# A two-bank PSUM tile becomes two one-bank tiles, allocated at each use

## The chip, the cores and the metric

The kernel runs on one core of one Trainium2 chip. The metric is the device time of one execution in microseconds (us), the median of several runs. A profile of one execution says where the time goes. The engines are TensorE (PE; its weight loads are PEld), VectorE (DVE), ScalarE (ACT), GpSimd (POOL) and SyncE (SP), which here only issues DMAs.

## The reference

Two branches work on 2048 tokens of 576 features and are mixed by a gate:

```python
g = sigmoid((x * gate_w).sum(-1, keepdims=True))
# branch A: a spectral filter
X = rfft2(x, axes=(-2, -1)) * (w_r + 1j * w_i)
a = irfft2(X, s=(2048, 576))
# branch B: a gated MLP, 576 -> 4608 -> 576
b = (gelu(x_b @ w_gate) * (x_b @ w_up)) @ w_down
out = g * a + (1 - g) * b
```

## The kernel before

*The MLP.* It is done in float32 precision by splitting each operand into a high and a low part and adding three products. The 4608 hidden features are 36 tiles of 128, taken in 18 pairs (j even, j odd); the tokens are two halves of two blocks (`tb`) of 512. For a hidden tile, `chain(j, s, tb)` adds 14 matmuls of 128x512 into one PSUM bank (512 float32 numbers a partition), for the gate (s=0) and for the up projection (s=1). `hidden` calls them one after the other: gate chain, `act.activation(..., Gelu_apprx_tanh)` on ScalarE out of the gate's bank (line 796), up chain, then VectorE's multiply out of the up's bank (`mult`, line 800), ScalarE's copy of the product to `hb` (high part) and VectorE's subtraction for the low part (line 804). `down` multiplies `hb` by `dn` (w_down) into the double tile `pdn`, 12 matmuls of 128x288 (line 818); ScalarE scales it to `stg` (line 843), and GpSimd issues a DMA that adds it to `yd` in DRAM. The downs of a hidden pair come one step later, four of them beside each pair of chains.

*The last stage.* For the second half of the tokens and the last 14 pairs of hidden tiles, `products` computes the gate and up projections by seven products of sums of blocks (Strassen's scheme) in place of eight. Each of the seven, n = 0 to 6, has two parts s of 7 matmuls (`seven`, lines 1013 to 1016), and VectorE adds each part out of PSUM to what it belongs to (`add`, line 1048). For odd n the parts go into `px`, by `ps_one()`, which takes the halves in turn; for even n into `pgu`.

*The transform.* The spectral filter runs in pieces beside the MLP: VectorE does the butterflies, and `columns` does DFTs over the columns by matmul (`product`, line 272, 6 matmuls of 128x290, three for each half al), between the chains, some 220 us from 350 on. There `wide[0]` is False and the chains use `pgu` alone; elsewhere the chains of an even j use `px`.

*PSUM.* There are eight banks: `pgu` is one bank in two buffers, `pdn` two banks in two buffers, and `px` one tile of two banks, allocated once at the beginning. `px` serves `first_chains` (the first pair), the chains of even j, the column products, the products of odd n, and `ps_one()` once more in `finale`.

*Order.* The order of instructions on each engine is that of the program text. `gap()`, called at fixed places in the chains, downs and products, emits queued work: steps due after so many gaps (`at`, `seq`), and pieces of the transform as far as a credit of estimated microseconds goes (`tick` adds what a chain takes on TensorE, the pieces subtract). Neither depends on measured time. The framework sets the semaphores: an instruction waits for those that touched the same tile before it, and where a tile is allocated anew under a name (tag), its first writer waits until the last tile in that buffer is free.

Of the kernel before, what the change touches and what calls it, by code (L numbers as in the profile page):

```python
# [10 lines left out]
F32 = mybir.dt.float32  # L11
F32R = mybir.dt.float32r
AF = mybir.ActivationFunctionType
ALU = mybir.AluOpType

P = 128
# [4 lines left out]
NK = KF + 1  # L21
# [4 lines left out]
TB = 512  # L26
# [132 lines left out]
def _build(nc, tc, a):  # L159
    with ExitStack() as ctx:  # L160
        ctx.enter_context(tc.manual_schedule())
        pool = ctx.enter_context(tc.tile_pool(name="sb", bufs=1))
        psum = ctx.enter_context(tc.tile_pool(name="ps", bufs=1, space=bass.MemoryType.PSUM))
        vec, act, pl, pe = nc.vector, nc.scalar, nc.gpsimd, nc.tensor

        def mk(n, shape, dt=F32):
            return pool.tile([P] + shape, dt, name=n, tag=n)
# [9 lines left out]
        gu = [mk(f"gu{i}", [2, KT, 256], F32R) for i in range(3)]  # L177
# [19 lines left out]
        def ps_gu():  # L197
            return psum.tile([P, TB], F32, name="pgu", tag="pgu", bufs=2)
# [1 line left out]
        def ps_dn():  # L200
            return psum.tile([P, 2, 512], F32, name="pdn", tag="pdn", bufs=2)

        px = psum.tile([P, 2, 512], F32, name="px", tag="px", bufs=1)
        ones = [0]

        def ps_one():
            ones[0] += 1
            return px[:, ones[0] % 2]

        def copy(o, i):  # L210
            act.activation(o, i, AF.Copy)  # L211
# [11 lines left out]
        def two(x):  # L223
            return x.rearrange("p (c k) -> p c k", c=2)[:, :, 0:NK]
# [3 lines left out]
        def columns():  # L228
# [5 lines left out]
            Z = [st[q] for q in turn]  # L234
# [4 lines left out]
            def cc(s, kb):  # L239
                q = 1024 * s + 512 * (kb % 2)  # L240
                return colm[:, q:q + 512]

            def load_cc(s, kb):
                if kb < 16:
                    pl.dma_start(cc(s, kb), a["col"][s, turn[kb]])

            def load_ww(kb):
                if kb < 16:
                    for c in range(2):
                        nc.sync.dma_start(ww[kb % 2][c], a["wf"][turn[kb], c])  # L250

            def corner(kb, slot, back):

                if not 0 <= kb < 16:
                    return
                z, c = two(Z[kb]), cns[:, slot + kb % 2]
                if back:
                    nc.sync.dma_start(z[0:64, 1], c[0:64])
                    nc.sync.dma_start(z[64:128, 0], c[64:128])
                else:  # L260
                    nc.sync.dma_start(c[0:64], z[64:128, 0])
                    nc.sync.dma_start(c[64:128], z[0:64, 1])

            def low(l, x, h):
                vec.tensor_tensor(l, x, f(h), ALU.subtract)

            def product(d, kb, h, l):
                v = px
                c = cc(d, kb).rearrange("p (a l k) -> p a l k", a=2, l=2)
                for al in range(2):  # L270
                    for n, (q, x) in enumerate(((0, h), (1, h), (0, l))):
                        pe.matmul(v[:, al, :NK], c[:, al, q], two(x)[:, al], start=n == 0, stop=n == 2)
                tick(6 * 0.135)
                load_cc(d, kb + 2)
                return v
# [48 lines left out]
            v = w = None  # L324
            for kb in range(18):
                on, was = kb < 16, 1 <= kb < 17
                if kb < 16:
                    z, (w0, w1) = two(Z[kb]), ww[kb % 2]
                    zr, zi = z[:, 0], z[:, 1]

                def filter_start():
                    vec.tensor_tensor(zi, v[:, 0, :NK], zr, ALU.subtract)
                    vec.tensor_tensor(zr, v[:, 0, :NK], zr, ALU.add)

                def swap():
                    act.activation(vs2[0:64], z[64:128], AF.Copy, scale=-1.0)
                    copy(vs2[64:128], z[0:64])

                def filter_end():
                    vec.tensor_tensor(z, z, two(vs), ALU.add)  # L340
                    vec.tensor_tensor(vs2[:, 0], zr, zi, ALU.add)
                    vec.tensor_tensor(vs2[:, 1], zr, zi, ALU.subtract)

                for g in range(STEP):
                    if g == 0:
                        while kb % 4 == 2 and kb < 14 and made[0] < kb // 4 + 1:
                            credit[0] -= next(side[0])
                        if on:
                            v = product(0, kb, xh, xl)
                            load_ww(kb + 1)  # L350
                            corner(kb + 2, 0, False)
                        if was:
                            copy(yh, vs)
                    elif g == 1:
                        if on:
                            copy(zr, v[:, 1, :NK])
                        if kb + 1 < 16:
                            copy(xh2, two(Z[kb + 1]))
                        corner(kb - 2, 2, True)
                    elif g == 2:  # L360
                        if on:
                            filter_start()
                        if was:
                            low(yl, vs, yh)
                    elif g == 3:
                        if on:
                            swap()
                            corner(kb + 2, 0, True)
                        if kb + 1 < 16:
                            low(xl2, two(Z[kb + 1]), xh2)  # L370
                    elif g == 4:
                        if was:
                            w = product(1, kb - 1, yh, yl)
                            copy(two(Z[kb - 1]), w[:, :, :NK])
                        if on:
                            vec.tensor_tensor(z, z, two(w0), ALU.mult)
                            vec.tensor_tensor(vs, vs, w1, ALU.mult)
                    elif g == 5:
                        if on:
                            filter_end()  # L380
                        if was:
                            corner(kb - 1, 2, False)
                    if kb == 17 and g > 4:
                        break
                    credit[0] -= 5.45 / STEP if on else 0.0
                    gone[0] = kb * STEP + g
                    yield None
# [254 lines left out]
        def tick(us):  # L642
            credit[0] += RATE * us
# [75 lines left out]
        def due(key):  # L719
            q = todo.pop(key, [])  # L720
            while q:
                q.pop(0)()
# [28 lines left out]
        wide = [True]  # L751

        def chain(j, s, tb):
            due(("gu", j))
            ps, w = px[:, s] if wide[0] and j % 2 == 0 else ps_gu(), gu[j % 3]
            c = slice(s * P, (s + 1) * P)
            for k in range(4):
                pe.matmul(ps, w[:, 0, k, c], xhi[tb][:, k], start=k == 0, stop=False)  # L758
                pe.matmul(ps, w[:, 1, k, c], xhi[tb][:, k], start=False, stop=False)  # L759
                pe.matmul(ps, w[:, 0, k, c], xlo[tb][:, k], start=False, stop=False)  # L760
                tick(3 * 0.2265)
                if k in (0, 2):
                    gap()
            pe.matmul(ps, w[:, 0, 4, c], xtl[tb], start=False, stop=False)  # L764
            pe.matmul(ps, w[:, 1, 4, c], xtl[tb], start=False, stop=True)  # L765
            tick(2 * 0.2265)
            return ps

        def first_chains():

            ps = [px[:, c] for c in range(2)]
            w, cs = gu[0], (slice(0, P), slice(P, 2 * P))
            for k in range(KT):
                for l, x in ((0, xhi), (1, xhi), (0, xlo)) if k < 4 else ((0, xtl), (1, xtl)):
                    for s in range(2):
                        x0k = x[0][:, k] if k < 4 else x[0]
                        pe.matmul(ps[s], w[:, l, k, cs[s]], x0k, start=k == 0 and l == 0 and x is xhi,
                                  stop=k == 4 and l == 1)
                tick(6 * 0.2265)
                if k < 4:  # L780
                    gap()
            return ps
# [237 lines left out]
        def products(i, spare, pend):  # L1020
# [31 lines left out]
            for n, (name, nd) in enumerate(zip(("a11", "a12", "s2", "s3", "s1", "a22", "s4"), downs)):  # L1052
# [9 lines left out]
                if n == 4:  # L1062
                    due(("dn", j))
                    due(("dn", j + 1))
                    load_d(i + 1)
                ps = [ps_one() if n % 2 else ps_gu() for _ in range(2)]
                for s in range(2):
                    seven(ps[s], i, n, name, s)
# [61 lines left out]
        ps = ps_gu()  # L1130
# [55 lines left out]
        for n in range(4 * NBLK):  # L1186
            p, r = divmod(n, 2 * NBLK)
            i, tb = divmod(r, 2)
            j = 2 * (p * NBLK + i)
# [21 lines left out]
            if state == 2 and tb == 1:  # L1211
                w = [g.rearrange("p l t k -> p (l t k)") for g in (gu[(j + 2) % 3], gu[j % 3], gu[(j + 1) % 3])]
# [95 lines left out]
```

## Time and profile before

| | |
|---|---|
| median of 3 runs | 1499.36 us (1496.73 to 1501.07) |
| profiled execution | 1502.38 us, span 1500.6 us |
| mean granted TensorE clock | 0.993 |
| PE busy | 1396.9 us of matmuls, 7490 of them |
| DVE busy | 1122.5 us |
| ACT busy | 701.7 us |
| POOL busy | 266.3 us |
| HBM | 118.56 MB read, 99.61 MB written |

The span is the time from the first to the last instruction on the core; the execution's own time is 1.8 us longer. Busy is the time in which an engine had an instruction in work. A matmul's row is longer than the distance to the next one's start, since matmuls are pipelined. In the rows of the timeline stand start (us), length (us), engine, line, operation, output<-input, shapes, count, and in brackets the idle time of the engine just ahead and what it waited for. In the rows of waits stand the engine with the waiting instruction's output and line, whom it waited for, and us in total, times, and the longest.

### The profile page before, as it was taken

What the parts mean: (1) busy time and instruction counts of PE and PEld (TensorE: products, weight loads), DVE (VectorE), ACT (ScalarE), POOL (GpSimd) and SP (SyncE); (2) the same over time, 40 slices, a digit from 0 to 9 for tenths busy, and PEclk for the clock granted to TensorE, in tenths of its full rate; (3) what the DMA queues carried; (4) which work ended last, traced back from release to release, by engine and by line L of the source; (5) the groups of instructions that cost most, each with busy time, mean ns of one, the idle gap of its engine ahead of it and who ended that gap; (6) DMA issues with size and microseconds to landing.
All of it is one profiled execution on the core that took longest, in us unless ns stands there. A gap on an engine that the chain in (4) does not pass through costs nothing. (4 is left out here: it accounts for less than half of the span.)

```text
span 1500.6 us, 20072 instructions
## 1 busy us (share of the span) xinstructions
PE 1396.9 (93%) x7490; PEld 1207.0 (80%) x7490; DVE 1122.5 (75%) x1649; ACT 701.7 (47%) x1079; POOL 266.3 (18%) x326
## 2 busy tenths in 40 slices
PE   9999999999999999999998989899999999999997
PEld 7778788888889878888887878777777787777787
DVE  6889798987877776998888841766666766666765
ACT  5443334355555664434644384444444444444441
POOL 0011111122222211111320022111111111111110
PEclk9999999999999999999999999999999999999999
DMA  9476655668999976557694777666665666666666
GB/s 335 160 177 140 146 118 96 113 124 192 216 237 271 249 153 124 106 105 141 129 280 139 202 155 121 147 121 118 119 120 111 108 114 110 106 114 121 115 133 158
DMA packets 102226, 226.65 MB, mean 151 GB/s; under 512 B 12400, under 2 KB 22640, under 8 KB 101744
## 3 DMA queue, kind: packets, MB, share of 16 engines
q0 software_dynamic: 45248, 92.56, 40.7%
q1 hardware_dynamic: 56880, 132.81, 28.1%
q8 instruction: 59, 0.97, 0.3%
q14 instruction: 39, 0.32, 0.1%
HBM read 118.56 MB, written 99.61 MB: 145 GB/s over the span
## 5 line engine op out<-in xcount | busy, mean ns | idle before, releaser
L831 POOL DMA_DIRECT2D yd<-stg x264 | 230.1, 872 | 1141.9 <-ACT stg L843 1101.4
L843 ACT ACTIVATE stg<-pdn,omg 128x576 f32<-128x576 f32 x272 | 201.9, 743 | 443.3 <-PE pdn L818 328.3
L818 PEld LDWEIGHTS pdn<-dn,hb 128*128 128x128 f32 x2760 | 382.1, 188 | 11.8 <-DVE raws L872 0.5
L818 PE MATMUL pdn<-dn,hb 128*128 128x288 f32 x2760 | 389.8, 295 | 0.2 <-DVE raws L872 0.2
L758 PE MATMUL pgu<-xhi,gu 128*128 128x512 f32 x440 | 172.8, 393 | 2.6 <-ACT gl L796 2.6
L759 PE MATMUL pgu<-xhi,gu 128*128 128x512 f32 x440 | 172.4, 392 | 0.4 <-DMA gu<-lo 0.4
L760 PE MATMUL pgu<-xlo,gu 128*128 128x512 f32 x440 | 172.1, 391 | 0.0
L758 PE MATMUL px<-xhi,gu 128*128 128x512 f32 x256 | 106.3, 415 | 37.3 <-ACT gl L796 37.3
L211 ACT ACTIVATE gu<-raws 128x1280 fp32r<-128x1280 f32 (+3 forms) x84 | 86.2, 1026 | 57.2 <-PE px L764 45.6
L759 PE MATMUL px<-xhi,gu 128*128 128x512 f32 x256 | 103.2, 403 | 0.0
L760 PE MATMUL px<-xlo,gu 128*128 128x512 f32 x256 | 102.8, 402 | 0.0
L760 PEld LDWEIGHTS pgu<-xlo,gu 128*128 128x128 f32 x440 | 83.0, 189 | 18.1
L758 PEld LDWEIGHTS pgu<-xhi,gu 128*128 128x128 f32 x440 | 83.0, 189 | 17.8 <-ACT gl L796 3.0
L758 PEld LDWEIGHTS px<-xhi,gu 128*128 128x128 f32 x256 | 49.5, 193 | 59.4 <-ACT gl L796 50.8
L759 PEld LDWEIGHTS pgu<-xhi,gu 128*128 128x128 f32 x440 | 83.0, 189 | 15.7 <-DMA gu<-lo 0.8
L818 PEld LDWEIGHTS pdn<-dn,gu 128*128 128x128 f32 x672 | 92.2, 188 | 2.1
L818 PE MATMUL pdn<-dn,gu 128*128 128x288 f32 x672 | 93.5, 295 | 0.0
L796 ACT ACTIVATE gl<-pgu 128x512 f32<-128x512 f32 x55 | 32.8, 597 | 125.5 <-PE pgu L765 111.8
L804 DVE TENSOR_TENSOR hb<-gl,hb 128x512 fp32r<-128x512 f32 x88 | 60.4, 686 | 40.9 <-ACT hb L211 40.6
L1048 DVE TENSOR_TENSOR xraw<-gl,px 128x512 f32<-128x512 f32 x56 | 38.5, 688 | 60.8 <-PE px L1016 58.3
L1013 PE MATMUL px<-xhi,gu 128*128 128x512 f32 x112 | 47.2, 421 | 27.3 <-DVE xraw L1048 27.3
L1031 DVE TENSOR_TENSOR xraw<-xraw 128x512 f32<-128x512 f32 x56 | 38.8, 693 | 31.5 <-ACT xraw L1039 30.9
(220 smaller groups left out, 2678.3 us busy)
## 6 DMA issues: line engine op xcount, KB each, us to landing
yd<-stg POOLq DMA_DIRECT2D x264, 288.0 KB, 5.0
raws<-wgu SPq DMA_DIRECT2D x42, 640.0 KB, 5.5
raws<-wd SPq DMA_DIRECT2D x72, 288.0 KB, 2.9
quads<-ws SPq DMA_DIRECT2D x24, 384.0 KB, 4.3
colm<-col POOLq DMA_DIRECT2D x32, 256.0 KB, 6.3
raws<-ws SPq DMA_DIRECT2D x21, 384.0 KB, 5.1
lo<-gu SPq DMA_DIRECT2D x8, 640.0 KB, 3.9
gu<-lo SPq DMA_DIRECT2D x8, 640.0 KB, 5.7
```

Of the source, the lines that this page charges most:

```text
L211: act.activation(o, i, AF.Copy)
L758: pe.matmul(ps, w[:, 0, k, c], xhi[tb][:, k], start=k == 0, stop=False)
L759: pe.matmul(ps, w[:, 1, k, c], xhi[tb][:, k], start=False, stop=False)
L760: pe.matmul(ps, w[:, 0, k, c], xlo[tb][:, k], start=False, stop=False)
L796: act.activation(g, pg, AF.Gelu_apprx_tanh)
L804: vec.tensor_tensor(h[:, 1], g, f(h[:, 0]), ALU.subtract)
L818: pe.matmul(ps[half], h[:, l, c], d[:, q, half * HD:(half + 1) * HD], start=part == 0 and n == 0, stop=part == 1 and n == 2)
L831: pl.dma_start(yd[u], o, accum_op=ALU.add)
L843: put(u, lambda o: act.activation(o.rearrange("p (c k) -> p c k", c=2), v[:, :, 0:HD], AF.Copy, scale=omg[:, u:u + 1]), i == 0)
L1013: pe.matmul(ps, hi[:, c], xh[:, t], start=t == 0, stop=False)
L1031: vec.tensor_tensor(v, g, v, ALU.mult)
L1048: vec.tensor_tensor(o, x, v, ALU.add)
```

## The change

The tile `px` of two banks goes. In its place `ps_x(c)` allocates a tile of one bank, under the name px0 or px1, at each use: for each chain of an even j, for the two halves of each column product, for each part of the products of odd n (by `ps_one`), and for the first pair. The banks used are the same two, in the same turns. A column product is now a list of two tiles, so ScalarE's copy of both halves in one instruction becomes two copies.

```diff
-        px = psum.tile([P, 2, 512], F32, name="px", tag="px", bufs=1)
+        def ps_x(c):
+            return psum.tile([P, TB], F32, name=f"px{c}", tag=f"px{c}", bufs=1)
+
         ones = [0]
 
         def ps_one():
             ones[0] += 1
-            return px[:, ones[0] % 2]
+            return ps_x(ones[0] % 2)
...
            def product(d, kb, h, l):
-                v = px
+                v = [ps_x(c) for c in range(2)]
...
-                        pe.matmul(v[:, al, :NK], c[:, al, q], two(x)[:, al], start=n == 0, stop=n == 2)
+                        pe.matmul(v[al][:, :NK], c[:, al, q], two(x)[:, al], start=n == 0, stop=n == 2)
...
-                    vec.tensor_tensor(zi, v[:, 0, :NK], zr, ALU.subtract)
-                    vec.tensor_tensor(zr, v[:, 0, :NK], zr, ALU.add)
+                    vec.tensor_tensor(zi, v[0][:, :NK], zr, ALU.subtract)
+                    vec.tensor_tensor(zr, v[0][:, :NK], zr, ALU.add)
...
-                            copy(zr, v[:, 1, :NK])
+                            copy(zr, v[1][:, :NK])
...
                             w = product(1, kb - 1, yh, yl)
-                            copy(two(Z[kb - 1]), w[:, :, :NK])
+                            for c in range(2):
+                                copy(two(Z[kb - 1])[:, c], w[c][:, :NK])
...
         def chain(j, s, tb):
             due(("gu", j))
-            ps, w = px[:, s] if wide[0] and j % 2 == 0 else ps_gu(), gu[j % 3]
+            ps, w = ps_x(s) if wide[0] and j % 2 == 0 else ps_gu(), gu[j % 3]
...
         def first_chains():
 
-            ps = [px[:, c] for c in range(2)]
+            ps = [ps_x(c) for c in range(2)]
```

Below, the order of instructions on an engine, with the semaphores that each waits for in brackets (by the engine that raises them; numbers after a name count buffers and tiles). First TensorE before, at the end of a gate chain in `px` and the beginning of the up chain (line 758), in the last quarter of the chains:

```order
L760 MATMUL px<-xlo_66,gu_72 128x512
L764 MATMUL px<-xtl_68,gu_72 128x512
L765 MATMUL px<-xtl_68,gu_72 128x512
L758 MATMUL px<-xhi_64,gu_72 128x512 [waits Activation_49]
L759 MATMUL px<-xhi_64,gu_72 128x512
```

and the same place now, where the lines are three further down (two tiles, px_5835 and px_5855):

```order
L763 MATMUL px_5835<-xlo_66,gu_72 128x512
L767 MATMUL px_5835<-xtl_68,gu_72 128x512
L768 MATMUL px_5835<-xtl_68,gu_72 128x512
L761 MATMUL px_5855<-xhi_64,gu_72 128x512 [waits DVE_49]
L762 MATMUL px_5855<-xhi_64,gu_72 128x512
```

The up chain's first matmul waited for ScalarE, whose latest instruction on `px` is the gelu of the gate chain just ended. Now it waits for VectorE, whose latest on that half is the multiply of the even hidden tile before. The matmuls stand where they stood.

Next, TensorE before, in the middle of a product of odd n, from the end of part s=0 to the beginning of part s=1 (line 1013 the second time):

```order
L1014 MATMUL px<-sx,gu_72 128x512
L1015 MATMUL px<-sx,gu_72 128x512
L1016 MATMUL px<-sx,gu_72 128x512 [waits DVE_49]
L1013 MATMUL px<-sx,gu_72 128x512 [waits DVE_49]
L1014 MATMUL px<-sx,gu_72 128x512
```

and now:

```order
L1017 MATMUL px_8578<-sx,gu_72 128x512
L1018 MATMUL px_8578<-sx,gu_72 128x512
L1019 MATMUL px_8578<-sx,gu_72 128x512 [waits DVE_49]
L1016 MATMUL px_8579<-sx,gu_72 128x512
L1017 MATMUL px_8579<-sx,gu_72 128x512
```

The wait of the second part for VectorE is gone; the one of line 1016 (now 1019) is for the weights' low part and stays.

Last, ScalarE in the column stage before, around the copy of a second product (`til<-px`):

```order
L336 ACTIVATE tmp<-til 64x580 [waits DVE_49]
L211 ACTIVATE tmp<-til 64x580
L211 ACTIVATE til<-px 128x580 [waits PE_49]
L211 ACTIVATE gu_72<-raws 128x1280 [waits DMAHW6_49]
L211 ACTIVATE colm<-tmp 128x580 [waits DVE_49,Activation_49]
```

and now:

```order
L338 ACTIVATE tmp<-til 64x580 [waits DVE_49]
L213 ACTIVATE tmp<-til 64x580
L213 ACTIVATE til<-px_3019 128x290 [waits PE_49]
L213 ACTIVATE til<-px_3020 128x290 [waits PE_49]
L213 ACTIVATE gu_72<-raws 128x1280 [waits DMAHW6_49]
L213 ACTIVATE colm<-tmp 128x580 [waits DVE_49,Activation_49]
```

One copy of 128x580 has become two of 128x290; the rest of ScalarE's order, and that of VectorE, GpSimd and SyncE, is the same in the whole program.

## The prediction

> **What bounds the kernel now.** I read first the busy times, then TensorE's own waits, then two places in the trace where these waits fall, then a table of the stretches between them. First the page's busy line:
>
> ```profile
> PE 1396.9 (93%) x7490; PEld 1207.0 (80%) x7490; DVE 1122.5 (75%) x1649; ACT 701.7 (47%) x1079; POOL 266.3 (18%) x326
> ```
>
> TensorE is the bound, and its idle time is 1500.6 - 1396.9 = 103.7 us. The waits of the PE engine (who was waited for: us in total, times, longest) say where most of it goes:
>
> ```profile
> PE px L1013 <- DVE xraw L1048: 48.3, 42, 1.7
> PE px L758 <- ACT gl L796: 37.3, 32, 4.7
> ...
> PE px L272 <- issue: 1.3, 2, 0.6
> PE px L272 <- ACT til L211: 1.2, 1, 1.2
> PE px L272 <- ACT stg L843: 1.0, 1, 1.0
> ...
> PE pgu L759 <- DMA gu<-lo: 0.4, 1, 0.4
> ```
>
> The first two rows are 85.6 us in 74 waits. Both are a matmul that starts a chain in `px` and waits for a reader of `px`. The timeline shows which half. First a chain pair (line 758 on), with the rows of VectorE and ScalarE that matter:
>
> ```profile
> 705.02 0.39 PE L765 MATMUL px<-xtl,gu 128*128 128x512 f32 x1
> 705.11 0.68 DVE L804 TENSOR_TENSOR hb<-gl,hb 128x512 fp32r<-128x512 f32 x1
> 705.50 0.60 ACT L796 ACTIVATE gl<-px 128x512 f32<-128x512 f32 x1 [1.42 <-PE px L765]
> ...
> 706.15 0.50 PE L758 MATMUL px<-xhi,gu 128*128 128x512 f32 x1 [0.75 <-ACT gl L796]
> ...
> 706.49 0.40 PE L759 MATMUL px<-xhi,gu 128*128 128x512 f32 x1
> ...
> 709.73 0.69 DVE L800 TENSOR_TENSOR gl<-gl,px 128x512 f32<-128x512 f32 x1 [1.46 <-PE px L765]
> ...
> 712.63 3.35 PE L818 MATMUL pdn<-dn,hb 128*128 128x288 f32 x24
> ```
>
> The gate chain (s=0) ends at 705.41 in half 0, ScalarE reads half 0 until 706.10, and only then does the up chain (s=1) start, in half 1. Half 1 itself was read last by VectorE's multiply (line 800); that comes 3.6 us after the up chain's start and once in a stretch of some 20 us, so the last one was about 16 us earlier. So TensorE waits for a half that it does not write. Then a product of the last stage:
>
> ```profile
> 1108.99 0.39 PE L1016 MATMUL px<-sx,gu 128*128 128x512 f32 x1
> ...
> 1110.12 0.69 DVE L1048 TENSOR_TENSOR xraw<-gl,px 128x512 f32<-128x512 f32 x1
> ...
> 1110.86 0.50 PE L1013 MATMUL px<-sx,gu 128*128 128x512 f32 x1 [1.48 <-DVE xraw L1048]
> ...
> 1111.20 0.39 PE L1014 MATMUL px<-sx,gu 128*128 128x512 f32 x1
> ```
>
> It is the same: the add reads the half of s=0, and the product of s=1 goes into the other half.
>
> **The change, part by part.** With a tile for each half, the order of instructions stays as it was on every engine but ScalarE (16 copies are split). The waits move: the up chain's first matmul now waits for VectorE's old multiply, the product's for nothing, as the order of TensorE in the section on the change shows. So the 74 waits as they stand go. What each is worth is more than its idle time. In the rows above matmuls start 0.23 us apart, though one lasts 0.39. From 705.02 to 706.49 are 1.47 us for two steps, so the stall costs 1.47 - 0.46 = 1.01 us, its idle time and 0.26 of refilling; in the product it is 2.21 - 0.46 = 1.75 against 1.48 idle, 0.27 more.
>
> *Products.* 42 stalls: 48.3 + 42 x 0.27 = 59.6 us.
>
> *Chains.* 32 stalls: 37.3 + 32 x 0.26 = 45.6 us. Four long ones cost more, since the clock falls behind them. The table of the stretches from one such stall to the next (us, then busy of PE, PEld, DVE, ACT, POOL, granted clock, DMA share, GB/s; of 30 rows the ones that matter, and the two sums) shows it:
>
> ```profile
> 45.31:67.07 21.76, 21.01 (x105) 17.94 (x105) 17.74 (x29) 9.07 (x14) 0.00 (x0) 0.92 0.40 142
> 67.07:87.22 20.15, 19.40 (x105) 16.80 (x105) 17.86 (x24) 9.66 (x15) 3.61 (x4) 1.00 0.67 190
> ...
> 108.80:128.94 20.14, 19.39 (x104) 16.80 (x104) 19.64 (x20) 7.11 (x11) 3.46 (x4) 1.00 0.67 142
> ...
> 171.53:193.29 21.76, 21.01 (x105) 17.93 (x105) 16.30 (x18) 7.04 (x11) 3.76 (x7) 0.92 0.75 198
> ...
> sum 290.21, PE 274.82 PEld 237.50 DVE 251.91 ACT 122.52 POOL 42.69; mean PE 19.63 PEld 16.96 DVE 17.99 ACT 8.75 POOL 3.05
> ```
>
> ```profile
> 625.63:645.77 20.14, 19.40 (x104) 16.79 (x104) 19.97 (x21) 7.11 (x11) 3.47 (x4) 1.00 0.58 108
> ...
> 811.97:834.83 22.86, 22.11 (x105) 18.73 (x105) 18.79 (x24) 6.89 (x10) 0.00 (x0) 0.87 0.40 135
> ...
> 899.31:921.06 21.75, 21.00 (x104) 17.93 (x105) 2.76 (x4) 11.57 (x14) 7.93 (x9) 0.92 0.87 155
> sum 335.74, PE 315.18 PEld 271.78 DVE 260.98 ACT 160.74 POOL 63.77; mean PE 19.70 PEld 16.99 DVE 16.31 ACT 10.05 POOL 3.99
> ```
>
> A plain stretch is 20.15 us, so 20.15 - 1.01 = 19.14 without its stall. The 14 stretches of the first sum and the 16 of the second last 625.95; 30 x 19.14 = 574.2; the difference is 51.8. The first stall of each group lies ahead of its sum and adds a plain one each, 2.0; the one wait for a DMA in there (0.4 + 0.26) is not the change's: 53.1 us, that is 45.6 and 7.5 for the clock. That full speed can be held without such pauses this row shows:
>
> ```profile
> 320.00:350.00 30.00, 30.00 (x174) 26.95 (x173) 26.88 (x41) 12.75 (x19) 8.27 (x11) 1.00 0.83 182
> ```
>
> The rows of the stalls that began the stretches with a low clock, and of one that did not:
>
> ```profile
> 45.31 0.50 PE L758 MATMUL px<-xhi,gu 128*128 128x512 f32 x1 [2.07 <-ACT gl L796]
> ...
> 108.80 0.50 PE L758 MATMUL px<-xhi,gu 128*128 128x512 f32 x1 [2.18 <-ACT gl L796]
> ...
> 171.53 0.50 PE L758 MATMUL px<-xhi,gu 128*128 128x512 f32 x1 [3.04 <-ACT gl L796]
> ...
> 811.97 0.80 PE L758 MATMUL px<-xhi,gu 128*128 128x512 f32 x1 [3.73 <-ACT gl L796]
> ...
> 899.31 0.53 PE L758 MATMUL px<-xhi,gu 128*128 128x512 f32 x1 [4.66 <-ACT gl L796]
> ```
>
> Pauses of 2.07 and 3.04 us were followed by a clock of 0.92, one of 2.18 was not. The Trainium skill (TensorE: Matmul & The Clock Gate, "HAM oscillation") gives the rule that no idle gap of TensorE should be longer than about 3.4 us. By it only the two longest stalls would cost clock, the 1.6 us each of the other two (21.76 - 20.15) would have another cause and stay, and the time would be 3.2 us higher. The trace does not agree with so high a threshold, so the sum keeps 53.1.
>
> *The split copies.* `product`'s second result is copied by ScalarE in two halves (16 times):
>
> ```profile
> L211 ACT ACTIVATE til<-px x32: 390/526/661, 359.2 to 564.1; 128x290 f32<-128x290 f32 x16, 128x580 f32<-128x580 f32 x16
> ```
>
> The shortest of these is 128x290, the longest 128x580 (ns): 2 x 0.39 - 0.66 = 0.12 us more each, 1.9 us in all, on an engine busy 47%. Against it, the next `product` may start when the first half is free; PE's waits of the column stage that could end on this are the 1.3 + 1.2 + 1.0 quoted above. I take 0 between -3.5 and +1.9.
>
> *What is late next.* TensorE gains about 1 us in 20, so VectorE must follow. In the stretch from 625.63 VectorE is busy 19.97, against 19.14 for TensorE: 0.8 us late there. What TensorE needs from it soonest is the low part of `hb` (line 804): done at 705.79, used from 712.63, 6.8 us ahead, and it moves 1 us nearer per stretch only while VectorE doesn't follow. From 590 to 690 VectorE's waits for TensorE were
>
> ```profile
> DVE gl L800 <- PE px L765: 2.3, 2, 1.3
> ```
>
> If of all its idle time only this can shrink, VectorE needs 97.7 us where TensorE would need 100 - 5 x 1.01 = 95.0: 2.7 late per 100. The two dense stretches (108 to 350, 585 to 850, some 500 us) then lose 13 us if nothing covers it, and nothing if the 6.8 us of margin in each hold. I take 0, since the work after them leaves VectorE free (2.76 of 21.75 from 899.31), and keep 13 as the other end. In the products VectorE is ahead of TensorE in most blocks, as its waits there say:
>
> ```profile
> DVE xraw L1048 <- PE px L1016: 86.0, 54, 2.0
> ```
>
> 86.0 us in 54 waits, 1.6 each, more than the 1.4 that a stall is worth (59.6 / 42), so I take 0. One place has another bound, the DMA engines:
>
> ```profile
> 750.00:770.00 20.00, 18.92 (x104) 16.38 (x103) 17.09 (x22) 9.10 (x14) 5.20 (x6) 1.00 1.09 266
> 770.00:790.00 20.00, 18.90 (x102) 16.06 (x101) 17.29 (x21) 8.05 (x12) 3.46 (x4) 1.00 1.00 287
> ```
>
> ```profile
> 747.47 0.50 PE L758 MATMUL px<-xhi,gu 128*128 128x512 f32 x1 [1.77 <-ACT gl L796]
> 768.00 0.50 PE L758 MATMUL px<-xhi,gu 128*128 128x512 f32 x1 [1.08 <-ACT gl L796]
> ```
>
> Their share is 1.0 there, and TensorE already waits 0.4 us for `gu<-lo`. I let that wait grow by the two stalls removed ahead of it, 1.77 + 1.08 + 2 x 0.26 = 3.4 us (ends: 0, and 4.4 with the next stall, a plain 1.01).
>
> *The sum*, against the profiled execution's 1502.4: 1502.4 - 59.6 - 53.1 + 0 + 0 + 3.4 = 1393.1. That execution is 3.0 above the median of the runs, so I give 1390 beside the median 1499.4, 7.3% less.
>
> **The rivals.**
> *A, VectorE becomes the bound in the transform stretches.* For it: 19.97 of 20.14 busy at 625.63. Against: the mean of the first sum is 17.99 per stretch, below 19.14. It gives back up to 13: 1403.
> *B, the chains give nothing*: ScalarE is what is late there (it reads at 705.50, and up to 4.66 us late), and TensorE, no longer held at line 758, meets the same lateness at line 818 in the evacuation of `pdn` or in `hb`. Against: 6.8 us of margin. It leaves the products alone: 1499.4 - 59.6 = 1440.
> *C, the change doesn't do what it says*: a tile allocated anew must wait until the last one of its name is free, and if that came as late as the reader of today, nothing would change: 1499. Against: the last reader of half 1 is 16 us old.
> *D, slower*: the short pauses gather. Without the hold at each chain, TensorE runs ahead until `hb` is not there, and waits once for several us at line 818; such a wait brings the low clock, 1.6 us each time. It decides if the idle time only moves and more than three pauses of over 2 us (4.5 us of lost clock) arise; with one in every five of the 74 stalls it costs 15 x 1.6 = 24: 1523. Against: the margins above.
> A reading of the page's idle time alone would remove 85.6 us: 1414. The Trainium skill (Trainium Kernel Development and Optimization, "Performance Expectations") says that matmul busy time is a bad metric, since matmuls are pipelined; the 0.39 us of a matmul that starts every 0.23 agree, and I stay with the distances between starts.
>
> **How the numbers follow.** Forecast 0.72, A 0.15, the idle-only reading 0.05, B 0.04, C 0.02, D 0.02. The range from 1378 to 1414 holds the first three: its low end is the sum with no DMA wait and with the columns' 3.5 (1383) and 5 for what differs from run to run, its high end the idle-only reading. Faster by over 0.3% (4.5 us, about what a measurement of this kernel can tell from no change): all but C and D, 0.96; within it C, 0.02; slower D, 0.02.
>
> **What would show it.** PE's waits at the chains' first matmul for ScalarE and at the products' for VectorE gone; PE idle below 25 us; the stretches from chain pair to chain pair near 19.1 us; a granted clock above 0.995; the 16 copies of 128x580 replaced by 32 of 128x290. I would be wrong if PE showed new waits at line 818's place for VectorE or ScalarE of more than 10 us, or stretches of 20 us in which VectorE is never idle.

## The result, and the profile after

The changed kernel takes 1390.03 us (median of 6 runs, 1387.69 to 1393.73), the kernel before in the same comparison 1499.72 us (6 runs, 1496.73 to 1502.40): a ratio of 0.9269, 95% interval 0.9251 to 0.9286. The forecast was 1390. The profiled execution took 1387.69 us, its span is 1385.8 and its granted clock 0.998.

The page's busy line of the changed kernel:

```profile
PE 1366.2 (99%) x7490; PEld 1206.0 (87%) x7490; DVE 1119.8 (81%) x1649; ACT 703.8 (51%) x1095; POOL 266.2 (19%) x326
```

TensorE is idle for 1385.8 - 1366.2 = 19.6 us, where it was 103.7. Its matmuls are also 30.7 us less busy, though they are the same 7490: a restart behind a stall and a low clock make single rows longer (0.50 us against 0.39 in the rows of the stalls), and most of those are gone. The waits of TensorE in the changed kernel (its lines stand two further down than before as far as the column stage, three behind that; in the kernels of the experiments an edit can move them by one or two more):

```profile
PE px L274 <- DVE colm L267: 4.0, 2, 2.3
PE pgu L762 <- DMA gu<-lo: 3.9, 1, 3.9
PE px L274 <- issue: 1.5, 2, 0.9
...
PE pgu L761 <- ACT gl L799: 1.1, 1, 1.1
...
PE px L274 <- ACT til L213: 0.7, 1, 0.7
```

Neither of the two great rows of before is left: no chain and no product of the last stage waits for a reader of px0 or px1 (the 0.7 us for `til` are a column product's). The timeline of a chain pair shows what took their place:

```profile
651.61 0.39 PE L768 MATMUL px<-xtl,gu 128*128 128x512 f32 x1
651.84 0.39 PE L761 MATMUL px<-xhi,gu 128*128 128x512 f32 x1
652.04 0.60 ACT L799 ACTIVATE gl<-px 128x512 f32<-128x512 f32 x1 [1.36 <-PE px L768]
652.07 0.39 PE L762 MATMUL px<-xhi,gu 128*128 128x512 f32 x1
...
653.43 0.69 DVE L807 TENSOR_TENSOR hb<-gl,hb 128x512 fp32r<-128x512 f32 x1
...
656.11 0.68 DVE L803 TENSOR_TENSOR gl<-gl,px 128x512 f32<-128x512 f32 x1
...
658.19 2.02 PE L821 MATMUL pdn<-dn,hb 128*128 128x288 f32 x14
```

The up chain's first matmul (651.84) comes 0.23 us after the gate chain's last (651.61), the usual distance, and the gelu reads px0 beside it. It is the same in the products (the last matmul of part s=0, the first of part s=1, then VectorE's add on the first part):

```profile
1025.19 0.39 PE L1019 MATMUL px<-sx,gu 128*128 128x512 f32 x1
...
1025.41 0.39 PE L1016 MATMUL px<-xhi,gu 128*128 128x512 f32 x1
...
1025.61 0.69 DVE L1051 TENSOR_TENSOR xraw<-gl,px 128x512 f32<-128x512 f32 x1 [0.39 <-PE px L1019]
```

A stretch from one up chain to the next in px1 (the columns are those of the stretches in the prediction) lasts 19.13 and 19.19 us in the two rows below, forecast 19.14, with TensorE busy in all of it:

```profile
613.52:632.65 19.13, 19.13 (x106) 16.90 (x105) 18.92 (x19) 6.95 (x10) 3.47 (x4) 1.00 0.61 112
632.65:651.84 19.19, 19.19 (x106) 16.93 (x105) 18.01 (x31) 10.77 (x21) 3.47 (x4) 1.00 0.61 113
```

VectorE paid for it with its slack. Its waits for the up chain of an even tile, before and after:

```profile
DVE gl L800 <- PE px L765: 50.7, 22, 7.5
```

```profile
DVE gl L803 <- PE px L768: 11.2, 9, 4.1
```

And it is nearer to being waited for. The low part of `hb` of the odd hidden tile, which the next downs need, is done at 654.12 above, and these downs start at 658.19, 4.1 us later; the same operation before was 5.1 us ahead (done at 687.44, downs from 692.49). The place that the prediction read, 6.8 us ahead, has 5.8 left (done at 671.50, downs from 677.29). It was not the narrowest one: four stretches earlier the downs came 3.6 us behind this operation before, and come 2.5 behind it now:

```profile
627.82 0.69 DVE L804 TENSOR_TENSOR hb<-gl,hb 128x512 fp32r<-128x512 f32 x1
...
632.11 3.35 PE L818 MATMUL pdn<-dn,hb 128*128 128x288 f32 x24
```

```profile
597.66 0.69 DVE L807 TENSOR_TENSOR hb<-gl,hb 128x512 fp32r<-128x512 f32 x1
...
600.87 3.35 PE L821 MATMUL pdn<-dn,hb 128*128 128x288 f32 x24
```

### The profile page after: what moved, and what is told of

The parts are those of the page before. It is cut to its first block, busy times and chain, and to the rows that moved or that the text cites. A ratio compares the mean times of both kernels' runs of the same rounds, so it can differ in the third digit from the quotient of the medians.

```text
span 1385.8 us, 20125 instructions
## 1 busy us (share of the span) xinstructions
PE 1366.2 (99%) x7490; PEld 1206.0 (87%) x7490; DVE 1119.8 (81%) x1649; ACT 703.8 (51%) x1095; POOL 266.2 (19%) x326
## 4 chain that ended last, share of the span: by engine, by line
PE 58%; DMA 1%; DVE 1%; ACT 0%; issue 0%; SPq 0%; DVEq 0%; ACTq 0%
PE pdn L821 20%; PE pgu L1016 4%; PE pgu L1018 4%; PE pgu L1017 4%; PE px L1016 3%; PE px L1018 3%; PE px L1017 3%; PE pgu L762 2%; PE pgu L763 2%; PE pgu L761 2%; PE px L761 2%; PE px L763 2%; PE px L762 2%; PE pgu L1019 2%; PE px L1019 1%; DMA gu<-lo 1%
## 5 line engine op out<-in xcount | busy, mean ns | idle before, releaser
L761 PE MATMUL px<-xhi,gu 128*128 128x512 f32 x256 | 100.0, 390 | 0.0
L763 PE MATMUL px<-xlo,gu 128*128 128x512 f32 x256 | 99.8, 390 | 0.0
L762 PE MATMUL px<-xhi,gu 128*128 128x512 f32 x256 | 99.7, 389 | 0.0
L1034 DVE TENSOR_TENSOR xraw<-xraw 128x512 f32<-128x512 f32 x56 | 38.8, 693 | 31.2 <-ACT xraw L1042 30.7
L1051 DVE TENSOR_TENSOR gl<-gl,pgu 128x512 f32<-128x512 f32 x56 | 38.3, 684 | 27.8 <-PE pgu L1019 27.8
L763 PEld LDWEIGHTS px<-xlo,gu 128*128 128x128 f32 x256 | 48.1, 188 | 10.4
L213 ACT ACTIVATE hb<-gl 128x512 fp32r<-128x512 f32 x88 | 54.9, 624 | 3.3 <-DVE gl L803 3.3
```

## The experiments

**Two tiles, allocated once.** The change has two halves: each bank becomes a tile of its own, and it is allocated at each use. This kernel does the first alone.

```diff
-        def ps_x(c):
-            return psum.tile([P, TB], F32, name=f"px{c}", tag=f"px{c}", bufs=1)
+        px = [psum.tile([P, TB], F32, name=f"px{c}", tag=f"px{c}", bufs=1) for c in range(2)]
+
+        def ps_x(c):
+            return px[c]
```

> Two tiles of one bank, allocated once at the beginning instead of anew at each use. Theory (what counts is that each bank is a tile of its own, so that a writer waits only for readers of its own bank): the same waits as with the change, 1390 us, within 4 of it; TensorE waits at the chains and products gone. Rival (the allocation at each use is what frees TensorE, by rotating): the 74 waits stay in part, 1440 to 1500 us.

Measured: 1391.14 us, before 1499.74 in the same comparison, ratio 0.927 (0.9253 to 0.9287). TensorE's waits are those of the changed kernel:

```profile
PE px L276 <- DVE colm L269: 4.0, 2, 2.3
PE pgu L764 <- DMA gu<-lo: 3.3, 1, 3.3
PE pgu L763 <- ACT gl L801: 2.5, 1, 2.5
```

So the tile of its own is the effect, and the fresh allocation adds nothing that these runs can tell (0.9270 against 0.9269).

**The chains undone.** Gate and up chain of an even tile both go into px0, so the up chain has a true reason to wait for the gelu.

```diff
-            ps, w = ps_x(s) if wide[0] and j % 2 == 0 else ps_gu(), gu[j % 3]
+            ps, w = ps_x(0) if wide[0] and j % 2 == 0 else ps_gu(), gu[j % 3]
```

> The chains alone undone: the gate and the up chain of an even hidden tile both use px0, so the up chain waits for the gelu again; products and columns as changed. Theory (a stall costs its idle time, 0.26 us of refilling, and 1.6 us of half clock behind the long ones; the DMA wait of 3.9 us at 736 shrinks to 0.4 again): 32 waits of 37 us in all, 1390 + 53 - 3.4 = 1440 us. Rival 1 (the idle time alone counts): 1390 + 37 = 1427 us. Rival 2 (the lateness of ScalarE would be met elsewhere anyway, the chains give nothing): 1390 us.

**The products undone.** Both parts of a product of odd n go into px1.

```diff
-                ps = [ps_one() if n % 2 else ps_gu() for _ in range(2)]
+                ps = []
                 for s in range(2):
+                    ps.append(ps_x(1) if n % 2 else ps_gu())
```

> The products alone undone: both parts of a product of odd n use px1, so the second part waits for VectorE's add on the first again; chains and columns as changed. Theory (42 stalls of 1.15 us idle and 0.27 of refilling, none long enough for the clock): 1390 + 59.6 = 1450 us, granted clock 0.997 or more. Rival (idle time alone): 1390 + 48 = 1438 us.

Measured: 1438.68 us with the chains undone (ratio to before 0.958, 0.956 to 0.960), 1451.45 with the products undone (0.9668, 0.9645 to 0.9692), beside the 1391.14 above. TensorE's waits in the first and in the second:

```profile
PE px L761 <- ACT gl L799: 37.6, 32, 4.7
```

```profile
PE px L1016 <- DVE xraw L1051: 48.3, 42, 1.7
...
PE pgu L762 <- DMA gu<-lo: 3.0, 1, 3.0
```

The chains are worth 47.5 us and the products 60.3, against 49.7 (53.1 less the 3.4 of the DMA) and 59.6 forecast; idle time alone would have been 37 and 48. Together they make 107.8 of the 108.6 between before and the kernel with two tiles, so the parts add up and little else is in the change. The profiled executions show the products' share without the spread between runs: from the first matmul of the last stage (at 937.1 us before, at 883.6 with the change) to the end they take 563.5 us before, 502.2 with the change, 502.3 with the chains undone and 563.0 with the products undone. The wait for `gu<-lo` is not in the list with the chains undone and is there with the products undone, as the account of it has it: only the stalls ahead of it in the chains matter to it.

**The load that became late.** In the changed kernel TensorE waits 3.9 us for one load. The rows of SyncE's issue and of the wait, and the windows before and in it:

```profile
718.17 0.51 SPq L733 DMA_DIRECT2D gu<-lo  x1
```

```profile
735.76 0.79 PE L762 MATMUL pgu<-xhi,gu 128*128 128x512 f32 x1 [3.93 <-DMA gu<-lo]
```

```profile
720.00:730.00 10.00, 10.00 (x56) 8.81 (x55) 9.47 (x11) 5.91 (x10) 3.46 (x4) 1.00 1.09 277
730.00:740.00 10.00, 6.07 (x21) 4.57 (x20) 7.11 (x10) 3.54 (x5) 0.00 (x0) 0.83 1.07 324
```

The load needed 17 us with the DMA engines full; the median of its eight loads is 6.1 us. Two kernels take it away: VectorE computes that one low part (hidden tile 37, counted on into the second half of the tokens), or all eight that are loaded, as it does in the first half. The changed kernel ran beside them once more. Of the two lines with a plus, the first stands in the one kernel and the second in the other:

```diff
-            if NT <= j < NT + 2 * FIRST:
+            if NT <= j < NT + 2 * FIRST and key != ("gu", NT + 1):   # one
+            if NT <= j < NT + 2 * FIRST and key[0] != "gu":          # all eight
```

> The changed kernel once more, on the chip of the next two runs, as their base: 1390 us, the DMA wait at about 736 us of 3 to 5 us.

> The changed kernel, but the low part of gu for hidden tile 37 (whose load from DRAM TensorE waits for at 736 us) is computed by VectorE instead: one load of 640 KB less in the stretch where the DMA engines are full, one operation of 1.5 us more on VectorE. Theory (that wait of 3.9 us, with 0.26 of refilling and 1.6 us of half clock, is the DMA engines' and nothing else is late): the wait gone, 1390 - 5 = 1385 us. Rival 1 (the DMA engines set the pace of the whole stretch, and the next load is late instead): 1388 to 1390 us, a wait for another load. Rival 2 (VectorE, busy 9.5 of 10 us there, becomes late): a new wait for VectorE of 1 to 2 us, 1387 us.

> The changed kernel, but all eight low parts of gu that were loaded from DRAM in the second half are computed by VectorE: eight loads of 640 KB less, 12 us more of VectorE between 690 and 840 us, where it is busy 127 of 160. Theory (VectorE has room there): no wait for a load, 1385 us, as with one computed. Rival (VectorE is the bound by then): it falls behind by several us and TensorE waits for it, 1388 to 1398 us.

Measured, beside a before of 1496.46: the changed kernel 1391.65 (0.9292, 0.9270 to 0.9315), one low part computed 1384.21 (0.9248, 0.9230 to 0.9265), all eight 1386.84 (0.9266, 0.9246 to 0.9287). With one computed there is no wait of TensorE between 690 and 850 us, and its windows at the same place read

```profile
720.00:730.00 10.00, 10.00 (x57) 8.70 (x56) 7.33 (x10) 4.96 (x8) 3.45 (x4) 1.00 1.09 277
730.00:740.00 10.00, 10.00 (x55) 8.82 (x55) 9.60 (x12) 4.58 (x7) 0.00 (x0) 1.00 1.07 256
```

The DMA engines are as full as before (1.07) and no other load comes late, so it was one late load and not their whole pace. The gain of 7.4 us is 2 more than the wait, its refilling and its clock; a wait for ScalarE at about 404 us, which the change doesn't touch and which lasted 1.1 to 3.6 us in the profiles of the changed kernel, is part of that difference between runs. With all eight computed TensorE waits 1.0 us for an evacuation instead; that it is the slower of the two isn't shown, the intervals overlap. The kernel with one has the lowest median of all here.

**Is VectorE the bound?** The low part of `hb` is computed twice, in chain stages and columns alike, so each hidden tile of each block costs VectorE some 0.65 us more (its busy time grows from 1119.8 to 1176.7 us, over 88 operations).

```diff
             def low():
-                vec.tensor_tensor(h[:, 1], g, f(h[:, 0]), ALU.subtract)
+                for _ in range(2):
+                    vec.tensor_tensor(h[:, 1], g, f(h[:, 0]), ALU.subtract)
```

> The changed kernel with VectorE's low part of hb computed twice per hidden tile in the chain stages (the same result): two more operations of 0.61 us in each stretch of 19.1 us. Theory (VectorE is not yet the bound; it is 4.1 us ahead of TensorE at its nearest between 570 and 690 us and busy 116.9 of 120 there): it falls behind by 4 to 5 us in that window, the margin covers most, TensorE waits 0 to 4 us: 1390 to 1395 us. Rival (VectorE is already the bound in the dense stretches, so each 1.2 us is paid): 13 to 20 stretches of 1.2 us, 1406 to 1414 us.

Measured: 1410.99 us (0.9399, 0.938 to 0.9418), 20 us more than the kernel with two tiles in the same comparison, the rival's number and not mine. TensorE's waits, those that are new or longer than in every profile of the changed kernel:

```profile
PE px L274 <- DVE colm L267: 5.8, 2, 3.4
PE pdn L822 <- ACT stg L847: 3.7, 1, 3.7
...
PE pgu L761 <- DVE gl L803: 3.0, 1, 3.0
PE pdn L822 <- DVE hb L808: 2.4, 6, 0.8
PE px L274 <- issue: 2.2, 2, 1.6
...
PE px L274 <- ACT til L213: 1.4, 1, 1.4
```

The mechanism is the rival's only in part. VectorE does fall behind until its margin at `hb` is used up; the 4.1 us that I took for the nearest between 570 and 690 us were 2.5 (the rows at 597.66 and 600.87 above). But what TensorE waits there is 2.4 us in six waits, and not 1.2 in each stretch. The rest is paid where the lateness reaches TensorE by another way: a `pgu` bank that VectorE had not yet read (3.0), the operands of the column products, and a `pdn` that ScalarE evacuates late since it waited for VectorE (3.7):

```profile
719.11 5.13 ACT L602 ACTIVATE til<-rows,gs 128x576 f32<-128x576 f32 x4 [7.18 <-DVE rows L444]
...
724.60 0.76 ACT L847 ACTIVATE stg<-pdn,omg 128x576 f32<-128x576 f32 x1
...
725.41 4.02 PE L822 MATMUL pdn<-dn,hb 128*128 128x288 f32 x17 [3.66 <-ACT stg L847]
```

These pauses are few and long, and the granted clock fell to 0.992, from 0.998 in the changed kernel. Two further kernels put the second operation only outside the column stage (`2 if wide[0] else 1`) and only in it, and a third doubles the like operation in the products.

> As the run with VectorE's low part of hb computed twice, but only outside the column stage: 66 more operations of 0.61 us (40 us of VectorE). Theory (VectorE is so near its limit there that it falls behind, and TensorE pays where a stretch ends on something late: 8.8 us up to the first column product and 7.6 us between the last one and 760 us by the trace of the run with all of them): 1391 + 16 = 1407 us. Rival 1 (the loss arises in the column stage, whose chain of VectorE, ScalarE and DMA is longer by each operation): 1391 to 1394 us. Rival 2 (each operation is paid): 1391 + 40 = 1431 us.

> The same, but only in the column stage: 22 more operations (13 us of VectorE). Theory: 7 us of the loss are there, 1398 us, in waits for VectorE's part of the columns and in the clock behind them. Rival 1: all 20 us, 1411 us. Rival 2 (VectorE is busy 173 of 222 us there and has room): 1391 us.

> The changed kernel with the low part of h computed twice in the products of the last stage: 56 more operations (34 us of VectorE), where VectorE is busy 386 of 535 us. Theory (VectorE has room there): 1391 us, within 3. Rival (the operation lies on the way to the first down of a block, which uses the low part at once: 0.6 us in each of 14 blocks): 1391 + 8 = 1399 us.

Measured: outside the columns 1405.62 us (0.9381, 0.9364 to 0.9398), in the columns 1397.34 (0.9326, 0.9311 to 0.9342), in the products 1396.26 (0.9316, 0.9302 to 0.9330). Against the 0.927 of the kernel with two tiles these are about 17, 8 and 7 us. No kernel without the second operation ran beside these three, and with the 0.9292 that the changed kernel had elsewhere they would be 13, 5 and 4. The first two lie near the theory of 16 and 7, and their sum near the 20 of both together, as far as this uncertainty lets one say. The third is not the theory's (no loss, within 3): from the first matmul of the last stage to the end, its profiled execution takes 509.2 us where the changed kernel takes 502.2, so the 7 us arise in the products. VectorE has room there, but the operation lies on the way to a block's first down. The waits there, and one of them:

```profile
PE pdn L821 <- DVE gu L1039: 2.8, 12, 0.3
```

```profile
951.10 1.41 DVE L1039 TENSOR_TENSOR gu<-xraw,gu 128x512 fp32r<-128x512 f32 x2
```

```profile
952.56 0.66 PE L821 MATMUL pdn<-dn,gu 128*128 128x288 f32 x3 [0.22 <-DVE gu L1039]
```

12 waits of 0.23 us with 0.26 of refilling each are 5.9 us. In the changed kernel the low part of the same block is done at 950.69, and the down's fifth matmul, the first that reads it, starts some 0.35 us later. That is less than one more operation takes (0.7 us, half of the 1.41 above). The theory that room on an engine covers a longer operation is wrong where the operation is awaited at once.

## Why the prediction was right

*The 74 waits wait for a half that isn't written.* Right: with each bank a tile of its own all 74 are gone, and a true reader in the same bank brings back 32 waits of 37.6 us and 42 of 48.3.

*A stall costs its idle time and 0.26 of refilling, and clock behind the long ones.* Right in size: 60.3 and 47.5 us measured by undoing, 59.6 and 49.7 worked out. The reading of the idle time alone fell short by 23 us (85.6 against 108.6), as the distance between starts had said. The 0.23 us between two starts can't be seen in the rows that the prediction quotes, which stand around a stall; the rows of the changed kernel show it (651.61 and 651.84).

*The clock.* The sum kept the clock as the trace had it. The Trainium skill (TensorE: Matmul & The Clock Gate, "HAM oscillation") gives the rule that no idle gap of TensorE should be longer than about 3.4 us; by it a pause of 2.07 us would cost no clock. With the chains undone the same pause of 2.07 us at 46.05 us is there again, and no low clock follows it:

```profile
46.05 0.50 PE L761 MATMUL px<-xhi,gu 128*128 128x512 f32 x1 [2.07 <-ACT gl L799]
```

```profile
46.00:66.00 20.00, 19.42 (x104) 16.80 (x104) 17.56 (x29) 8.96 (x14) 0.00 (x0) 1.00 0.43 155
```

So of the 7.5 us that I booked for the clock, 1.6 hung on the luck of that one execution. The Trainium skill says elsewhere on that page (TensorE: Matmul & The Clock Gate, "What's actually happening") that the window in which activity is counted is not tied to the kernel's start; the same pause with and without a low clock agrees with that, though no run here shows the window itself.

*The load at 736 us grows by 3.4.* It grew by 3.5 (0.4 to 3.9 of idle time). What I left out is the clock behind it (0.83 in its window), some 1.6 us more.

*The split copies cost nothing.* The 48 copies of 128x290 together took about 1 us more of ScalarE, and TensorE's waits in the column stage for colm, issue, til and stg are 4.0, 1.5, 0.7 and 0.2 us where they were 4.0, 1.3, 1.2 and 1.0:

```profile
L213 ACT ACTIVATE til<-px x48: 387/406/417, 335.4 to 536.4; 128x290 f32<-128x290 f32 x48
```

*VectorE follows.* Right for the change: no wait of TensorE for `hb` is in the profile, though VectorE is busy 97% of the time between 570 and 690 us (116.92 of 120):

```profile
570.00:690.00 120.00, 120.00 (x656) 106.11 (x656) 116.92 (x143) 51.70 (x81) 23.07 (x27) 1.00 0.66 126
```

But the reason I gave, one margin of 6.8 us, was read at a wide place (3.6 us at 628, above) and was too narrow a reason. The run with more work on VectorE shows that `hb` is not the only place where its lateness is met, and that some 0.65 us more per hidden tile already costs 20. The change asks for 1 us in 20, and VectorE's waits for TensorE shrank (50.7 us before, 11.2 after), so it seems to have had that much to give; no run shows this by itself.

*The time itself.* The forecast of 1390 met the median of 1390.03 more closely than its terms deserve: undone, the chains come out 2.2 us below their term (the clock behind the load and behind the pause of 2.07 us are 1.6 each), the products 0.7 above, and single executions of the changed kernel lie up to 6 us apart. That closeness is luck; the two large terms are not.

Of the rivals, A did not come about, as no new wait of TensorE for VectorE is in the dense stretches. B is excluded by the run with the chains undone, which loses 47.5 us where B has it lose nothing, C by the profile, and D didn't come about: no pause at the downs of more than 0.2 us is left.

## What to carry to other kernels

When an engine waits at the start of a write, look in the timeline at which part of the tile the reader reads: if it is another bank than the one written, two tiles are worth more than the idle time shows, since each stall also costs its refilling (0.26 us here) and a long one some clock (1.6 us here). Work out such a gain from the distance between starts, and ask of every engine near its limit by which ways its lateness reaches the bound one, not by the nearest way alone. A stretch whose DMA engines are full can give back some of what is gained just ahead of it, as with the load here; one operation moved from the DMA to an engine took that back.

## What the runs showed of the hardware that was not expected

Pauses of TensorE between 2.06 and 2.9 us were followed by a half clock in 10 of 26 cases over the twelve profiles here, those of 2.97 us and more in 19 of 19, and shorter ones in one case (1.61 us, 9 us behind a pause of 2.42). A stretch of 21.76 us at a mean clock of 0.92 means, as an estimate, some 3.5 us at half clock; it lasted 1.6 us longer than the plain one of 20.15. Behind the wait at 735.76 matmuls start 0.43 us apart, elsewhere 0.23. So in the runs of this kernel a pause of a little over 2 us may or may not bring the low clock, and one of 3 us did each time.
